# q and k loads in 2 KB packets, turned into token order, and a recorded emission order, in a fused attention and FFN kernel

## The chip, the cores and the metric

The kernel runs on one core of a Trainium2 chip. The metric is the device time of one execution in microseconds (us). The time before is 300.6 us, the median of three runs (299.19, 300.60 and 301.54 us).

A core has five instruction streams that matter here: PE (TensorE, matrix products; PEld is its weight load), DVE (VectorE), ACT (ScalarE), POOL (GpSimd) and SP (SyncE, which here only issues DMAs). Each stream is carried out in the order in which the program emits it; streams wait for each other by semaphores.

## The reference

Attention with a choice of key chunks, then an RMS norm and a gated FFN. Inputs q, k, v are (4, 8, 768, 64) float32: 4 batches, 8 heads, 768 tokens, 64 features.

```python
k_chunks = k.reshape(B, H, nc, 32, D)                 # nc = 24 chunks of 32 tokens
k_min = np.min(k_chunks, axis=3); k_max = np.max(k_chunks, axis=3)
ub = np.sum(np.maximum(q[:, :, :, None, :] * k_min[:, :, None, :, :],
                       q[:, :, :, None, :] * k_max[:, :, None, :, :]), axis=-1)
ub = np.where(causal_by_chunk, ub, -1000000000.0)
top_chunks = np.argsort(ub, axis=-1)[..., -6:]        # six chunks per query
scores = scale * np.matmul(q, k.transpose(0, 1, 3, 2))
scores = np.where(sel & causal, scores, -1000000000.0)
attn = softmax(scores)
out = np.matmul(attn, v)                              # then (B*S, H*D) = (3072, 512)
...
xn = x / rms * rms_g
g = xn @ w_gate                                       # (512, 1536)
silu = g * (1.0 / (1.0 + np.exp(-g)))
return (silu * (xn @ w_val) @ w_out)                  # (1536, 512)
```

## The kernel before

**Tiling.** The 3072 tokens are cut into 12 blocks of 256: a pair (b, m) of batch and place in the sequence, taken in the order of the list `ORDER` ((0,0), (1,0), (2,0), (3,0), (0,1), (1,1), (0,2), (2,1), (1,2), (3,1), (2,2), (3,2)). The eight heads are two groups g of four. A block is attended in two jobs (one for each g) and then passes through the FFN in six pieces of 256 hidden columns, for its 256 rows.

**A job.** SP loads k and q of a block (`load_qk`, issued in line 528) into `kraw` and `qraw`: four heads lie on the four groups of 32 partitions, and a partition holds eight tokens. DVE turns each 32x32 square (line 794, `STREAM_TRANSPOSE`) so that features lie on partitions: `kT`, `qT`. ACT or POOL makes bf16 copies `kb`, `qb` (`half`, lines 801 and 802). DVE takes the smallest and the largest of each chunk (`ext`, line 809, into `kx`). For blocks with m > 0, four DMAs issued by SP cross halves of `qT` into `QX` (line 864); `relu` (line 888) writes into the used `qraw`. PE makes the upper bounds (`upper`, lines 680 and 698), DVE finds the sixth largest and the mask (lines 723 to 755). PE makes scores (line 922) and adds the mask by a product with `chunkrow` (line 933), ACT takes exp (line 972), POOL cuts the triangle (line 942), PE multiplies by v (`values`, line 998), and DVE normalises (lines 1013, 1017).

**Norm and FFN.** ACT squares (line 1034), POOL makes the inverse root (lines 1040, 1042). For the first four blocks PE transposes x; for the other eight a DMA transposition issued by SP does (line 1058, `xsT<-xs`). PE multiplies by `wg` and `wv` (line 1122), ACT takes tanh and copies (lines 1129, 1141), DVE and POOL multiply (lines 1133, 1137, 1144), PE projects with `wo` (line 1169), and the result is stored by SP (line 1191).

**Two layouts of a load.** Blocks 0 to 2 of `ORDER` are in the set `PACKED`: a partition gets eight tokens that follow each other in memory, one packet of 2 KB per head; four loads of 128 KB for k and four for q. The turn then leaves the tokens out of order in `kT` and `qT` (position j*32 + r holds token 8r + j), and `half`, `ext`, `relu` and `upper_first` read or write with strides to set that right. In the other nine blocks partition r gets the tokens j*32 + r, in packets of 256 bytes: eight loads of 64 KB for k and eight for q, and `kT`, `qT` are in token order.

**The order of the work.** The functions do not emit at once. They make operations (`plan.op`) with an engine or a choice of engines (`flex`), an occupancy and a latency in us, and what they read, write and take from a pool of buffers. `Plan.run` then places them: at each step it takes the operation that can start first on its engine, by the due times in the list `DUE`, with a model of the DMA queues in the class `Rings`; buffers of some pools are taken in a fixed order. Where PE would stand idle in the first 60 us of the plan it adds products whose result is not used (`keep_busy`, line 1245), 77 with 128 columns and 39 with 512. Each engine's stream, SP's too, is emitted in the order that comes out. The first weight loads wait for `dk(0, 0, 0)`; the loads of block 2 and 3 wait for parts of the weights (`HELD`).

Of the kernel before, what the change touches and what calls it, by code (L numbers as in the profile page):

```python
# [19 lines left out]


# [15 lines left out]
class Rings:  # L37
    FETCHED = 3.3

    def __init__(self):  # L40
        self.now = 0.0
        self.queue = {}
        self.wait = []

    def _step(self, until):
        while True:
            heads = [q[0] for q in self.queue.values() if q]
            nxt = self.wait[0][0] if self.wait else None
            if not heads:
                if nxt is None or nxt > until:  # L50
                    return
                self.now = max(self.now, nxt)
            else:
                cycle = sum(d[1] for d in heads)
                end = self.now + min(d[0] for d in heads) * cycle
                stop = min(end, until, nxt if nxt is not None else end)
                if stop > self.now:
                    for d in heads:
                        d[0] -= (stop - self.now) / cycle
                    self.now = stop  # L60
                for q in self.queue.values():
                    if q and q[0][0] <= 1e-9:
                        q[0][2](self.now)
                        q.pop(0)
            while self.wait and self.wait[0][0] <= self.now + 1e-12:
                _, ring, d = self.wait.pop(0)
                ahead = sum(x[0] * x[1] for x in self.queue.get("POOL", ()))
                if ring != "POOL" and not d[3] and ahead > 0.0 and not self.queue.get(ring):
                    d[3] = True
                    self.wait.append((self.now + min(self.FETCHED, ahead), ring, d))  # L70
                    self.wait.sort(key=lambda w: w[0])
                    continue
                self.queue.setdefault(ring, []).append(d)
            if self.now >= until and not (self.wait and self.wait[0][0] <= until):
                if not any(q and q[0][0] <= 1e-9 for q in self.queue.values()):
                    return

    def add(self, t, ring, packets, cost, op):
        self._step(min(t, self.wait[0][0]) if self.wait else t)

        def landed(now, op=op):
            op.done = now + (0.9 if op.dma[2] else 1.2) + op.slack
        op.done = None
        self.wait.append((t, ring, [packets, cost, landed, False]))
        self.wait.sort(key=lambda w: w[0])
        self.guess()

    def room(self, ring, t):

        other = Rings()  # L90
        other.now = self.now
        other.queue = {r: [list(d) for d in q] for r, q in self.queue.items()}
        other.wait = [(w, r, list(d)) for w, r, d in self.wait]
        for q in list(other.queue.values()) + [[d for w, r, d in other.wait]]:
            for d in q:
                d[2] = lambda now: None

        def held():
            return sum(d[0] for d in other.queue.get(ring, ())) + sum(
                d[0] for w, r, d in other.wait if r == ring)  # L100

        while held() > 85.0:
            t = max(t, other.now) + 0.25
            other._step(t)
        return t

    def guess(self):
        other = Rings()
        other.now = self.now
        other.queue = {r: [list(d) for d in q] for r, q in self.queue.items()}  # L110
        other.wait = [(t, r, list(d)) for t, r, d in self.wait]
        other._step(1e9)


class Plan:

    SHARES = ("qx", "scale", "relu", "bd0", "bd1", "dk", "mk")
    PATIENT = {"DVE": 0.6, "ACT": 0.6}  # L120
    STICK = 25
    RESERVED = ("hh",)
    HOP = {"PE": 0.055, "ACT": 0.04, "DVE": 0.04, "POOL": 0.075, "SP": 0.06}

    DUE = (
        150, 162, 271, 116, 142, 170, 90, 156, 806, 900, 1138, 1422, 80, 161, 167, 163, 185, 185, 186, 186,
        187, 187, 187, 188, 12, 188, 188, 189, 200, 190, 191, 192, 194, 195, 80, 79, 85, 84, 91, 91, 95,
        122, 165, 161, 180, 195, 185, 190, 210, 214, 111, 218, 286, 225, 234, 140, 157, 160, 172, 180, 183,
        185, 155, 154, 146, 162, 202, 209, 216, 219, 216, 136, 173, 177, 183, 197, 201, 202, 206, 208, 212,
        225, 175, 178, 201, 203, 219, 229, 224, 241, 232, 235, 242, 278, 282, 19, 199, 223, 230, 235, 241,  # L130
        245, 248, 252, 240, 188, 191, 196, 202, 258, 264, 274, 278, 244, 254, 257, 282, 293, -22, 275, 280,
        299, 315, 299, 307, 323, 344, 340, 392, 213, 221, 233, 251, 249, 260, 361, 341, 333, 240, 266, 265,
        276, 294, 304, 321, 272, 291, 251, 280, 305, 310, 322, 305, 389, 293, 306, 297, 318, 320, 337, 346,
        -18, 341, 349, 401, 323, 308, 317, 470, 353, 364, 343, 392, 408, 441, 428, 418, 429, 441, 315, 328,
        336, 357, 360, 22, 358, 398, 405, 328, 327, 343, 367, 373, 385, 401, 411, 413, 417, 429, 428, 436,
        469, 414, 433, 427, 444, 395, 431, 380, 363, 357, 376, 576, 426, 404, 409, 419, 438, 456, 451, 445,
        512, 467, 476, 525, 510, 514, 463, 421, 466, 501, 417, 502, 797, 489, 379, 503, 514, 423, 411, 515,
        454, 474, 479, 484, 489, 488, 491, 506, 565, 500, 515, 501, 523, 523, 539, 514, 560, 542, 552, 561,
        472, 408, 414, 515, 518, 530, 522, 537, 575, 549, 505, 557, 567, 572, 590, 578, 597, 592, 607, 565,
        564, 571, 610, 678, 683, 641, 903, 465, 468, 490, 495, 500, 458, 507, 512, 518, 520, 530, 536, 541,  # L140
        267, 548, 553, 573, 588, 547, 819, 573, 585, 615, 619, 621, 609, 653, 567, 778, 591, 597, 607, 623,
        625, 588, 654, 618, 622, 605, 683, 682, 637, 772, 707, 760, 777, 729, 737, 736, 747, 744, 761, 784,
        786, 770, 793, 795, 660, 763, 867, 768, 791, 753, 792, 813, 818, 797, 823, 829, 900, 807, 792, 862,
        870, 883, 1080, 598, 559, 563, 569, 574, 579, 584, 659, 667, 676, 682, 688, 693, 629, 704, 711, 843,
        874, 711, 755, 727, 732, 704, 758, 864, 738, 721, 790, 738, 750, 770, 741, 798, 764, 1009, 740, 796,
        804, 745, 823, 852, 1096, 780, 891, 889, 792, 875, 892, 1020, 1031, 969, 980, 1000, 992, 1006, 1002,
        1013, 1024, 1022, 1247, 1055, 1026, 1130, 1060, 1079, 1030, 1042, 1046, 1051, 1052, 1044, 1055,
        1066, 1077, 1083, 1090, 1085, 1094, 1101, 1111, 1117, 1126, 1136, 1151, 1143, 1163, 726, 732, 738,
        744, 748, 759, 767, 773, 811, 766, 817, 827, 833, 838, 848, 854, 1028, 1044, 817, 955, 811, 871,
        945, 912, 1085, 956, 835, 954, 855, 903, 947, 845, 959, 934, 1179, 960, 998, 1009, 975, 987, 1027,  # L150
        1030, 1015, 1028, 1034, 1040, 1060, 1067, 1080, 1181, 1090, 1104, 1180, 1130, 1186, 1138, 1147,
        1158, 1193, 1217, 1219, 1193, 1372, 1222, 1225, 1186, 1194, 1217, 1213, 1222, 1222, 1002, 1251,
        1261, 1268, 1273, 1266, 1281, 1282, 1257, 1324, 1288, 1311, 1321, 1318, 1333, 864, 879, 895, 903,
        910, 828, 930, 936, 955, 964, 976, 987, 860, 1002, 1008, 1021, 1211, 1242, 980, 1107, 996, 1006,
        943, 1089, 1269, 1088, 990, 1134, 1018, 1027, 1070, 1072, 1064, 1219, 1075, 1080, 1122, 1134, 1128,
        1158, 1164, 1170, 1183, 1223, 1224, 1244, 1222, 1266, 1363, 1317, 1329, 1342, 1326, 1355, 1346,
        1363, 1379, 1278, 1294, 1306, 1387, 1326, 1441, 1405, 1453, 1450, 1452, 1380, 1373, 1433, 1407,
        1437, 1416, 1429, 1440, 1455, 1478, 1488, 1504, 1518, 1525, 1510, 1531, 1539, 1565, 1574, 1536,
        1594, 1633, 1586, 1627, 1040, 1038, 1038, 1033, 1041, 1047, 1053, 1059, 1064, 1075, 1086, 1092,
        1103, 1098, 1109, 1115, 1460, 1455, 1084, 1415, 1110, 1122, 1147, 1159, 1319, 1167, 1104, 1364,  # L160
# [94 lines left out]
    def run(self, in_order=(), fill=None):  # L255
# [19 lines left out]
        def offer(o):  # L275
            for e in o.alts:
                cand[e].append(o)
# [1001 lines left out]
```

## Time and profile before

| | |
|---|---|
| median of 3 runs | 300.6 us |
| span of the profiled execution, first to last instruction | 297.4 us |
| granted TensorE clock, mean | 0.997 |
| first product that is not fill, last PE product | at 9.15 us, at 293.7 us |
| DMA packets, under 512 B of them | 86388, 74816 |
| DMAs issued by SP | 262 |

The span is one profiled execution. No other time is given for that execution; the median of the timed runs lies 3.2 us above its span. A number such as "128x512" is partitions by elements. Busy time of an engine is the time in which an instruction runs; the ends of PE's products are modelled, so a busy PE is not always at its peak rate. "Waited for" names what came last before an engine went on; a wait for several semaphores is put down to one of them.

### The profile page before, as it was taken

To read this page: it belongs to the slowest core of one execution; us is meant where nothing else is said; L and a number is where in the kernel's file an instruction comes from. 1 tells how busy PE (TensorE), PEld (TensorE's weight loads), DVE (VectorE), ACT (ScalarE), POOL (GpSimd) and SP (SyncE) were. 2 spreads that over 40 slices of the span, in tenths; PEclk is the share of its full clock that TensorE was granted. 3 is DMA by queue.
4 is the path that set the end of the run, shared out by engine and by line. 5 is a ranking of instruction groups with operands and counts; after the bars stand their busy time and mean duration, and the time that the engine had idled before them with its cause. 6 is when DMAs were issued, how large, how long until landed. Compare 5 with 4: busy or idle time off the path is not lost.

```text
span 297.4 us, 11418 instructions
## 1 busy us (share of the span) xinstructions
PE 282.5 (95%) x4672; PEld 213.4 (72%) x4672; DVE 217.1 (73%) x623; ACT 216.7 (73%) x372; POOL 155.6 (52%) x266
## 2 busy tenths in 40 slices
PE   7879999999999996999999999899999999999994
PEld 7548777657858854878767787488688778678763
DVE  6987774977998998888999999679356454456430
ACT  4897877688979876987985797677587668565331
POOL 4885858755976864475583276538044114214120
PEclk9999999999999999999999999999999999999998
DMA  7999998755676656654768576511014021011011
GB/s 188 208 204 206 255 197 163 159 130 134 141 194 154 144 136 103 149 100 110 205 135 162 108 193 150 133 40 39 0 57 55 1 82 30 2 73 35 2 71 71
DMA packets 86388, 35.08 MB, mean 118 GB/s; under 512 B 74816, under 2 KB 81728, under 8 KB 86336
## 3 DMA queue, kind: packets, MB, share of 16 engines
q1 hardware_dynamic: 80736, 29.12, 42.6%
q0 software_dynamic: 4752, 4.72, 9.4%
q8 instruction: 36, 0.59, 0.8%
q10 hardware_dynamic: 848, 0.53, 0.7%
q14 instruction: 16, 0.13, 0.2%
HBM read 28.58 MB, written 6.29 MB: 117 GB/s over the span
## 4 chain that ended last, share of the span: by engine, by line
PE 76%; DMA 9%; DVE 4%; ACT 4%; SPq 3%; POOL 1%; issue 1%; DVEq 0%; POOLq 0%; ACTq 0%
PE F L1122 39%; PE F L1169 18%; PE S L922 6%; PE F L998 6%; PE F L680 3%; SPq L528 3%; PE S L933 2%; DMA xsT<-xs 2%; DMA qraw<-in_q_dram 2%; DMA vraw<-in_v_dram 2%; DMA kraw<-in_k_dram 2%; DVE kx L809 1%; POOL hh L1144 1%; DVE m L739 1%; ACT th L1129 1%
## 5 line engine op out<-in xcount | busy, mean ns | idle before, releaser
L972 ACT ACTIVATE pt<-S 128x1024 bf16<-128x1024 f32 (+3 forms) x104 | 85.6, 857 | 19.7 <-PE S L933 18.2
L1144 POOL TENSOR_TENSOR hh<-tg,vs 128x512 bf16<-128x512 bf16 x48 | 55.7, 1164 | 42.6 <-ACT vs L1141 22.9
L1133 DVE SCALAR_TENSOR_TENSOR tg<-th,F 128x512 bf16<-128x512 bf16 x72 | 48.4, 680 | 39.3 <-ACT th L1129 33.7
L1122 PE MATMUL F<-xsT,wg 128*128 128x256 bf16 (+1 forms) x608 | 72.6, 267 | 3.7 <-DVE xnat L1017 1.7
L1122 PE MATMUL F<-xsT,wv 128*128 128x256 bf16 (+1 forms) x608 | 72.4, 267 | 0.6 <-DMA xsT<-xs 0.3
L1169 PE MATMUL F<-wo,hh 128*128 128x512 bf16 (+1 forms) x300 | 68.5, 371 | 1.8 <-POOL hh L1144 0.6
L1122 PEld LDWEIGHTS <-wg 128*128 128x128 bf16 x608 | 55.6, 98 | 13.5 <-issue 2.7
L1122 PEld LDWEIGHTS <-wv 128*128 128x128 bf16 x608 | 55.2, 98 | 9.7 <-DMA vraw<-in_v_dram 0.8
L1129 ACT ACTIVATE th<-F 128x512 bf16<-128x512 f32 x72 | 42.5, 598 | 19.7 <-PE F L1122 17.4
L942 POOL TENSOR_SCALAR_AFFINE_SELECT pt<-pt 128x512 bf16<-128x512 bf16 x48 | 32.2, 674 | 32.3 <-ACT pt L972 31.7
L1169 PEld LDWEIGHTS <-hh 128*128 128x128 bf16 x300 | 27.7, 98 | 28.4 <-issue 1.8
L1141 ACT ACTIVATE vs<-F 128x512 bf16<-128x512 f32 x48 | 28.7, 598 | 13.2 <-PE F L1122 10.1
L922 PE MATMUL S<-qb,kb 32*128 32x256 bf16 (+1 forms) x800 | 32.8, 253 | 2.3 <-ACT qb L801 2.0
L809 DVE TENSOR_REDUCE kx<-kT 128x16 f32<-128x512 f32 x48 | 30.4, 664 | 0.0
L998 PEld LDWEIGHTS <-pt 128*128 128x128 bf16 x672 | 24.8, 98 | 3.1 <-issue 0.3
L998 PE MATMUL F<-VX,pt 128*128 128x65 bf16 x672 | 26.6, 194 | 0.2 <-ACT vs L1141 0.2
L922 PEld LDWEIGHTS <-kb 32*128 32x128 bf16 x800 | 13.9, 92 | 15.0 <-issue 14.4
L933 PE MATMUL S<-mtd,chunkrow 32*128 32x128 bf16 (+2 forms) x384 | 20.5, 203 | 0.2 <-issue 0.2
L933 PE MATMUL S<-mto,chunkrow 32*128 32x128 bf16 (+2 forms) x384 | 19.9, 203 | 0.0
L1017 DVE TENSOR_TENSOR xnat<-F,rden 128x256 bf16<-128x256 f32 x48 | 19.2, 415 | 0.7
L933 PEld LDWEIGHTS <-chunkrow 32*128 32x128 bf16 x768 | 18.5, 93 | 1.2 <-issue 0.4
L1034 ACT ACTIVATE junk<-xnat 128x512 bf16<-128x512 bf16 x24 | 15.1, 631 | 5.4 <-DVE xnat L1017 5.0
(71 smaller groups left out, 337.2 us busy)
## 6 DMA issues: line engine op xcount, KB each, us to landing
vraw<-in_v_dram SPq DMA_DIRECT2D x24, 256.0 KB, 4.4
out_dram<-osb SPq DMA_DIRECT2D x23, 256.0 KB, 2.4
kraw<-in_k_dram SPq DMA_DIRECT2D x72, 64.0 KB, 2.4
qraw<-in_q_dram SPq DMA_DIRECT2D x72, 64.0 KB, 2.2
QX<-qT SPq DMA_DIRECT2D x32, 64.0 KB, 2.7
wg<-in_moe_w_gate_dram POOLq DMA_DIRECT2D x3, 512.0 KB, 12.3
wv<-in_moe_w_val_dram POOLq DMA_DIRECT2D x3, 512.0 KB, 14.3
wo<-in_moe_w_out_dram POOLq DMA_DIRECT2D x3, 512.0 KB, 23.5
```

What stands on the lines that cost most here:

```text
L809: plan.op(f"ext{n}{J}", "DVE", 0.585, 0.67, lambda n=n, op=op: VE.tensor_reduce(out=at(kx)[:, g, n], in_=at(kT).rearrange("p h (j c x) -> ...
L922: TE.matmul(s[a // 2][:, a % 2, c0:c0 + q1 - q0], kbt[r, t, ks], qbt[r, t, q0:q1], start=(t == 0), stop=(t == 1 and not mask), skip_group_ ...
L933: TE.matmul(o, chunkrow[r, BLK * kg + P * e:BLK * kg + P * (e + 1)], mv, start=False, stop=(d == 1), skip_group_check=True)
L942: GE.affine_select(out=d, in_=d, compare_op=ALU.is_ge, fill=0.0, base=0, pattern=[[0, 4], [1, P]], channel_multiplier=-1)
L972: lambda pt=pt, hs=hs, c0=c0, c1=c1, x=sc[hp]: SE.activation(out=at(pt)[:, hs, c0:c1], in_=at(x)[:, :, c0:c1], func=ACT.Exp, scale=SCALE), ...
L998: TE.matmul(o[:, a, :], p_[:, a, off:off + P], vt[:, e, a, :], start=(kb_ == 0 and a == 0), stop=(kb_ == nkb - 1 and a == 3), skip_group_c ...
L1122: TE.matmul(at(p_)[:, n * W:(n + 1) * W], w[:, g, ht * P:(ht + 1) * P], at(xT)[:, g, x0:x0 + W], start=(g == 0), stop=(g == NP - 1), skip_ ...
L1129: plan.op(f"tanh{U}.{hp}", "ACT", 0.48, 0.6, lambda th=th, gp=gp: SE.activation(out=at(th), in_=at(gp), func=ACT.Tanh, scale=0.5), pri - 0 ...
L1133: VE.scalar_tensor_tensor(out=at(tg), in0=at(th), scalar=1.0, in1=at(gp), op0=ALU.add, op1=ALU.mult), pri - 30, reads=[th, gp], writes=[tg ...
L1141: plan.op(f"vcopy{U}.{hp}", "ACT", 0.48, 0.6, lambda vs=vs, vp=vp: SE.activation(out=at(vs), in_=at(vp), func=ACT.Copy), pri + 0.1, reads= ...
L1144: plan.op(f"hh{U}.{hp}", "POOL", 1.11, 1.16, lambda tg=tg, vs=vs, hh=hh: GE.tensor_tensor(out=at(hh), in0=at(tg), in1=at(vs), op=ALU.mult) ...
L1169: TE.matmul(at(op)[:, cs], at(key)[:, o:o + P], wo[:, ht, cs], start=(ht == 0), stop=(ht == NHT - 1), skip_group_check=True)
```

## The change

Three things change.

1. `PACKED` is gone: all 12 blocks load q and k in the layout with 2 KB packets, in four loads of 128 KB each (before: three blocks). Counted over the program, loads of q and k go from 168 to 96, and SP's DMAs from 262 to 190.
2. The turn writes its output with a stride of 8 elements (32 bytes), so that `kT` and `qT` are in token order. The strided accesses of `half`, `ext`, `relu` and `upper_first` go; these now read and write in order.
3. `Rings`, `DUE` and the placing are gone. A list `SEQUENCE` gives the order of all 1508 operations (1580 before), `SLOTS` the buffer of each, `CHOICE` the engine of each `flex` operation, and `WARM` where fill goes: again 77 products with 128 columns and 39 with 512. Some occupancies are other numbers than before; nothing reads them any more in the changed kernel.

In the emitted streams, 73 `flex` operations change their engine; the net change is 6 more operations on DVE, 3 fewer on ACT, 3 fewer on POOL. PE's 315 operations are the same, in another order: 55 stand at the same place, 141 within three places of it. The changes between PE's kinds of operation (FFN and values, scores, upper bounds) go from 121 to 132.

```diff
+SEQUENCE = [
+    34, 19, 35, 3, 37, 36, 33, 0, 21, 6, 23, 32, 16, 31, 8, 4, 1, 38, 7, 17, 25, 30, 9, 15, 40, 10, 18, 42, 20,
...
+SLOTS = [
...
+CHOICE = (
...
+WARM = [
+    (60, 77, 0, 0), (72, 4, 0, 1), (99, 6, 0, 1), (120, 8, 2, 1), (126, 2, 2, 1), (135, 4, 3, 1), (146, 2, 0,
+    1), (158, 2, 3, 1), (174, 1, 2, 1), (242, 6, 3, 1), (258, 4, 1, 1)]
...
-    PACKED = {0, 1, 2}
...
-            if i in PACKED:
-                sv = src[b].rearrange("(g a) (m r j) d -> a m r g (j d)", a=4, m=NBLK, r=32)[a, m]
-                todo = [(sv, lambda rows=rows: at(key)[rows].rearrange("r g j h d -> r g (j h d)"),
-                         4, 0.104 if i == 0 else 0.12)]
-            else:
-                todo = []
-                for g in range(NG):
-                    sv = src[b, 4 * g + a, BLK * m:BLK * (m + 1), :].rearrange(
-                        "(j r) d -> r j d", r=32)
...
+            sv = src[b].rearrange("(g a) (m r j) d -> a m r g (j d)", a=4, m=NBLK, r=32)[a, m]
+            dma(f"load {nm}{b}{m}{a}", eng, sv,
+                lambda rows=rows: at(key)[rows].rearrange("r g j h d -> r g (j h d)"),
...
-                    lambda: VE.transpose(out=turned(nm).rearrange("p h (j r) -> p j h r", r=32, j=8),
+                    lambda: VE.transpose(out=turned(nm).rearrange("p h (r j) -> p j h r", r=32, j=8),
                                          in_=at(raw)[:, g]),
...
-            act = lambda: SE.activation(out=natural(at(hb)), in_=order(turned(nm)), func=ACT.Copy)
-            pool = lambda: GE.tensor_copy(natural(at(hb)), order(turned(nm)))
+            act = lambda: SE.activation(out=at(hb), in_=turned(nm), func=ACT.Copy)
+            pool = lambda: GE.tensor_copy(at(hb), turned(nm))
...
-                out=at(kx)[:, g, n], in_=at(kT).rearrange("p h (j c x) -> p h c j x", j=8, x=4)
-                if packed else at(kT).rearrange("p h (c t) -> p h c t", t=CH),
-                axis=AXXY if packed else AXX, op=op), base + 1, reads=[kT, kT + (g,)] + ([kx] if n or g else []), writes=[kx + (g, n)],
+                out=at(kx)[:, g, n], in_=at(kT).rearrange("p h (c t) -> p h c t", t=CH),
+                axis=AXX, op=op), base + 1, reads=[kT, kT + (g,)] + ([kx] if n or g else []), writes=[kx + (g, n)],
...
-    for o in plan.run(in_order=("kraw", "qraw", "vraw", "kT", "qT", "kb", "qb", "QX", "VX", "xsT", "xs", "hh", "xnat"),
-                      fill=(1.6, 5.6, 60.0, 0.0565, 0.216, "F", keep_busy)):
+    for o in plan.run(("F", keep_busy)):
         o.fn()
```

In the new order SP issues the four DMAs of line 864 for block (1, 1) one right after the other, directly before the loads of block (2, 1), and the first DMA transposition (line 1058) stands behind 118 DMAs (before: 138).

## Prediction

> **What bounds the kernel now.** First the page: how busy each engine is, and where. These are the busy times, then PE's and the DMAs' rows of the span in 40 slices, then the chain that ended last.
>
> ```profile
> PE 282.5 (95%) x4672; PEld 213.4 (72%) x4672; DVE 217.1 (73%) x623; ACT 216.7 (73%) x372; POOL 155.6 (52%) x266
> ...
> PE   7879999999999996999999999899999999999994
> ...
> DMA  7999998755676656654768576511014021011011
> ...
> PE 76%; DMA 9%; DVE 4%; ACT 4%; SPq 3%; POOL 1%; issue 1%; DVEq 0%; POOLq 0%; ACTq 0%
> ```
>
> PE bounds it: 76% of the chain, and no other engine is near 95%. The change takes no product away from PE, so it can only win time in which PE waits or does fill. The view by stretches says where that is (columns: length, then busy us of PE, PEld, DVE, ACT, POOL; clock; DMA share).
>
> ```profile
> 9.00:60.00 51.00, 47.98 (x827) 35.10 (x829) 39.11 (x123) 41.55 (x86) 39.05 (x69) 1.00 1.06 198
> 60.00:140.00 80.00, 75.44 (x1357) 57.29 (x1356) 69.96 (x230) 66.93 (x119) 52.21 (x76) 1.00 0.59 136
> 140.00:195.00 55.00, 54.13 (x1064) 39.53 (x1062) 49.45 (x152) 43.78 (x70) 29.83 (x52) 1.00 0.66 149
> 195.00:294.00 99.00, 98.48 (x1363) 75.22 (x1354) 52.10 (x110) 59.52 (x95) 30.14 (x36) 1.00 0.14 39
> 75.00:187.50 112.50, 108.08 (x2041) 81.95 (x2038) 104.21 (x330) 92.03 (x154) 71.34 (x111) 1.00 0.64 144
> ```
>
> PE's idle time is 51.00 - 47.98 = 3.0 us at first, 4.6 us from 60 to 140, 0.9 us and 0.5 us after that: 9.0 us in all. In the first stretch it also makes 39 wide fill products; five that follow each other take 1.24 us with 0.38 us for the last, so 0.215 us each and 8.4 us in all. The pool is thus some 17 us, half of it fill that the changed program makes again (39 of the same size). From 195 us on there is nothing to win. The clock is full throughout.
>
> What holds PE in the second stretch is read from the chain between 100 and 136 us.
>
> ```profile
> 104.72 0.59 SPq L864
> 105.37 0.58 SPq L528
> ...
> 108.46 0.45 SPq L528
> 108.96 0.59 SPq L864
> 109.59 0.59 SPq L864
> 110.23 2.06 DMA QX<-qT
> 112.53 0.62 POOL qraw L888
> 113.20 1.15 PE F L680 x45
> ...
> 131.32 3.72 DMA xsT<-xs
> ```
>
> SP's queue is in it: between the first and the last of four crossings (line 864) SP issues six loads of q, then the crossings land, POOL makes relu, and PE stands idle 0.4 us before line 680. The two DMA transpositions are issued behind all that, from 112.08 to 114.7 us, and at 117.58 us PE begins line 1122 after 1.7 us idle (the profile's list names DVE there, but the weight load of the same products waited for `xsT<-xs`). At 135.1 us the next transposition is late too.
>
> **Part 1: fewer and larger loads.** 72 DMAs of SP go. A load's issue takes 0.449 us (median of 82 for k), so 72 x 0.449 = 32 us of SP's time between 40 and 175 us, in which the timeline shows SP issuing almost without a pause. Crossings, transpositions and stores behind loads go out sooner, and SP's order puts the crossings of block (1, 1) together. The price: a load of 64 KB lands 2.4 us after its issue, one of 128 KB 5.3 us, though that figure is from the start, with a DMA share of 1.06. At a share of 0.6 I take 3 us; loads stand many microseconds ahead of their turn, so it costs nothing unless a turn follows closely (+1 us at most, for two such places). Gain: bounds 0 (the waits come back elsewhere) and the 4.6 + 0.9 us of idle time in these stretches. I take 3.5 us, most of it, because 0.4 + 1.7 us of it hang on SP by the chain, and the smaller ones at 129.8 and 135.1 us follow the late transposition.
>
> **Part 2: the copies read in order.** In blocks 0 to 2 the twelve copies to bf16 read with a stride of 128 bytes. One view by source line gives the prices (minimum/median/maximum ns).
>
> ```profile
> L801 ACT ACTIVATE kb<-kT x14: 612/637/1115, 5.8 to 163.7; 128x512 bf16<-128x512 f32 x14
> L801 ACT ACTIVATE qb<-qT x8: 610/1083/1147, 8.0 to 113.9; 128x512 bf16<-128x512 f32 x8
> ...
> L794 DVE STREAM_TRANSPOSE qT<-qraw x24: 668/694/712, 7.3 to 176.8; 128x512 f32<-128x512 f32 x24
> ...
> L809 DVE TENSOR_REDUCE kx<-kT x48: 642/672/687, 6.3 to 185.3; 128x16 f32<-128x512 f32 x48
> ```
>
> The strided ones are the 1083 ns, the others 637 ns: 0.446 us less each. On the path lie the one before the first scores (9.15 us, PE had waited 1.06 us for it) and the three between 15 and 22.5 us, where ACT is busy 7.50 of 7.50 us. Bounds: 0.45 us (the first alone) and 4 x 0.446 = 1.8 us. I take 1.0 us: the fill stays in PE's stream, and DVE's chain to the first norm is not shortened. The loads of block 3 (issued from 40 to 53 us) go from packets of 256 bytes to an eighth as many, but between 40 and 60 us PE hardly idles: 7.50 and 7.46 of 7.50 us in the two stretches from 45 us on. Nothing for that. `ext`, with one or two free axes, has 642 to 687 ns in both layouts: nothing.
>
> **Part 3: the turn writes with a stride of 32 bytes.** The trace has no such turn. Its nearest rows: `ext` reads pieces of 16 bytes, 128 bytes apart, at the price of plain reading; and DVE's small memset (line 730) writes float32 with a step of 136 bytes, 16 of them in 72 ns against 2 in 60 ns, so 12 / 14 = 0.86 ns an element, less than the turn's 694 / 512 = 1.36 ns. By these the cost is 0. The other bound is ACT's stride, 0.446 us a turn. Nothing suggests a gain, since the reading side is unchanged. I take 0, for the memset is DVE's own writing with a larger step.
>
> [...]
>
> **Part 4: the order.** PE's kinds of work change 132 times instead of 121. In the trace line 922 begins 0.10 us later after line 1122 than the latter's spacing of 0.110 us would give (100.26 against 99.83 + 3 x 0.110). So 11 x 0.10 = 1.1 us more. Six operations move to DVE net, most of them `dk` (0.325 us there): 2 us of DVE, hidden while it has 8.3 us to spare in 75 to 187.5 us. The last products (the projection of block 11 in halves) stand as before, so the tail is kept. New waits of the order: between -1 and +5 us, from the pool's 9.0 us of idle time that the old order left; I take 0, as most PE operations stand within three places.
>
> **Sum.** 297.4 - 3.5 - 1.0 + 0 + 1.1 + 0 = 294.0 us of span; with the 3.2 us by which the median lies above the span, 297.2 us. Two of the bounds lie further down than up of what I took (0.9 us more of idle time, 0.8 us of ACT), so I put the forecast a little lower, at 296.7 us.
>
> **The rivals.** *The moves cancel.* PE is at 95%, its fill is the same, and each wait removed may stand again a few products later, in the new order. For it: after 140 us PE idles only 1.4 us, so nearly all must come from the 4.6 us before. Then 300.6 + 1.1 - 1.0 gives 300.7 us, from 298.5 to 303.
>
> *DVE becomes the bound (slower).* If a turn costs 0.446 us more, the four of block 0 stand before the first bounds and scores: 4 x 0.446 = 1.8 us. From 75 to 187.5 us there are 28 turns: 12.5 us more, against DVE's idle time of 112.5 - 104.2 = 8.3 us, so at least 4.2 and at most 12.5 us. With the 3.4 us of the sum's gain off, 300.6 - 3.4 + 6.0 = 303.2 to 300.6 - 3.4 + 14.3 = 311.5 us. It decides from 8.3 / 28 = 0.30 us a turn on. For it: ACT's row; DVE is 93% busy in that stage. Against it: the memset and `ext`.
>
> *The relief is larger.* If SP's queue also caused what is put down to DVE and ACT between 60 and 100 us and half of the start's waits, up to 9.0 us of idle time goes: 300.6 - 9.0 + 1.1 = 292.7 us.
>
> **How the numbers follow.** Forecast 0.40 (294.5 to 298.5 us), larger relief 0.12 (290.5 to 294.5), moves cancel 0.26, DVE the bound 0.22. About 1%, 3 us, is what a measurement of this kernel can tell from no change. Faster by over 1% (below 297.6 us): 0.33 of the forecast and 0.12 make 0.45. Slower by over 1% (above 303.6 us): 0.21 of DVE and 0.04 of the moves make 0.25. Within 1%: 0.30. The range reaches from 291 to 306 us: it leaves out the lowest of the relief and the upper half of the DVE case. The forecast's own range is 294.5 to 298.5 us.
>
> **What would show it.** Line 801 at 0.64 us in all rows; line 794 still near 0.69 us (at 1.0 us or more the slower rival is right); SP with 190 DMAs and pauses between 60 and 175 us; no idle time of PE over 0.5 us before lines 680 and 1122 between 100 and 140 us; PE's idle time from 60 to 195 us near 2 us instead of 5.5 us. It would be wrong if PE's idle time there is unchanged, or if loads that land later than 3 us hold up turns.

## The result, and the profile after

The changed kernel takes 310.6 us (median of 4 runs, 309.6 to 312.4), the kernel before 299.9 us beside it (299.1 to 301.5). The ratio is 1.033, with a 95% interval from 1.027 to 1.039. It is slower by some 10 us; the forecast was 296.7 us. The profiled execution has a span of 309.2 us.

The page first, with the rows shown of before and DVE's row in the 40 slices.

```profile
PE 288.0 (93%) x4672; PEld 216.8 (70%) x4672; DVE 237.3 (77%) x628; ACT 210.5 (68%) x367; POOL 155.3 (50%) x263
...
PE   8599989979999988898799999999999999999994
...
DVE  7689986999998999999989999984635643645251
...
PEclk9879999988999999999999999999999999999999
...
PE 52%; DVE 29%; DMA 8%; issue 4%; ACT 3%; SPq 2%; POOL 1%; DVEq 0%; ACTq 0%; POOLq 0%
```

DVE's row and the row of the clock that TensorE was granted (PEclk, in tenths) were these before:

```profile
DVE  6987774977998998888999999679356454456430
...
PEclk9999999999999999999999999999999999999998
```

DVE has taken over: its share of the chain that ended last goes from 4% to 29%, at PE's cost, and it is at nine tenths in most slices up to the 26th. Two dents in PEclk are new, at slices 2 and 3 and at 9 and 10. The view by stretches shows the same in us (columns: length, then busy us of PE, PEld, DVE, ACT, POOL; clock; DMA share; GB/s).

```profile
9.00:60.00 51.00, 46.39 (x783) 33.25 (x783) 43.99 (x121) 36.29 (x76) 34.52 (x59) 0.93 1.07 204
60.00:140.00 80.00, 74.14 (x1280) 55.41 (x1279) 76.79 (x229) 63.90 (x117) 54.25 (x87) 0.98 0.71 172
140.00:195.00 55.00, 50.55 (x914) 37.93 (x912) 52.20 (x137) 40.19 (x65) 29.09 (x46) 1.00 0.32 82
```

From 60 to 195 us DVE is busy 129.0 of 135 us (before: 119.4), and PE idles 10.3 us where it idled 5.4 us. What DVE does more is read from the view by source line (minimum/median/maximum ns).

```profile
L594 DVE STREAM_TRANSPOSE kT<-kraw x24: 1079/1102/1167, 5.2 to 186.0; 128x512 f32<-128x512 f32 x24
L594 DVE STREAM_TRANSPOSE qT<-qraw x24: 1070/1096/1122, 10.1 to 179.0; 128x512 f32<-128x512 f32 x24
...
L601 ACT ACTIVATE qb<-qT x10: 630/630/668, 11.3 to 188.1; 128x512 bf16<-128x512 f32 x10
```

Line 594 is the turn, line 794 of before. It takes 1.10 us where it took 0.69 us: 0.41 us more, 48 times, is 19.7 us of DVE. ACT's copies are at 0.63 us throughout, as Part 2 said. The list of PE's waits between 9 and 195 us names the same engine (columns: us in total, times, longest).

```profile
PE S L717 <- ACT qb L601: 4.0, 2, 3.7
PE F L917 <- DVE tg L928: 3.1, 5, 0.9
PE F L917 <- DVE xnat L812: 1.9, 2, 1.1
PE F L506 <- DVE tg L928: 1.4, 1, 1.4
PE F L917 <- DVE xsT L886: 1.0, 1, 1.0
```

Only the first row is another matter: the first scores stand at 11.95 us instead of 9.15 us. In the new order ACT's table load (1.28 us, from 1.72 us on) stands ahead of ACT's two loads of q, which go out at 4.08 instead of 1.73 us. I had not looked at ACT's queue at the start when I costed the order.

### The profile page after: what moved, and what is told of

Its sections match the earlier page's. It is cut to its first block, busy times and chain, and to the rows that moved or that the text cites. A ratio compares the mean times of both kernels' runs of the same rounds, so it can differ in the third digit from the quotient of the medians.

```text
span 309.2 us, 11305 instructions
## 1 busy us (share of the span) xinstructions
PE 288.0 (93%) x4672; PEld 216.8 (70%) x4672; DVE 237.3 (77%) x628; ACT 210.5 (68%) x367; POOL 155.3 (50%) x263
## 4 chain that ended last, share of the span: by engine, by line
PE 52%; DVE 29%; DMA 8%; issue 4%; ACT 3%; SPq 2%; POOL 1%; DVEq 0%; ACTq 0%; POOLq 0%
PE F L917 25%; PE F L964 14%; DVE qT L594 5%; DVE kT L594 5%; PE S L717 4%; PE F L793 4%; DVE kx L609 4%; DVE tg L928 4%; DMA kraw<-in_k_dram 3%; DVE xnat L812 2%; DVE xs L847 2%; DMA qraw<-in_q_dram 2%; SPq L349 2%; DMA vraw<-in_v_dram 2%; PE S L728 1%
## 5 line engine op out<-in xcount | busy, mean ns | idle before, releaser
L939 POOL TENSOR_TENSOR hh<-tg,vs 128x512 bf16<-128x512 bf16 x48 | 56.8, 1189 | 44.5 <-DVE tg L928 25.8
L964 PE MATMUL F<-wo,hh 128*128 128x512 bf16 (+1 forms) x300 | 69.9, 376 | 1.7 <-DVE tg L928 0.9
L964 PEld LDWEIGHTS <-hh 128*128 128x128 bf16 x300 | 28.3, 99 | 28.9 <-issue 4.2
L737 POOL TENSOR_SCALAR_AFFINE_SELECT pt<-pt 128x512 bf16<-128x512 bf16 x48 | 30.7, 648 | 16.3 <-ACT pt L767 16.0
L717 PE MATMUL S<-qb,kb 32*128 32x256 bf16 (+1 forms) x800 | 33.5, 255 | 4.2 <-ACT qb L601 4.0
L793 PEld LDWEIGHTS <-pt 128*128 128x128 bf16 x672 | 25.8, 98 | 6.2 <-issue 2.3
L793 PE MATMUL F<-VX,pt 128*128 128x65 bf16 x672 | 28.3, 194 | 1.7 <-DVE xnat L812 0.8
L594 DVE STREAM_TRANSPOSE qT<-qraw 128x512 f32<-128x512 f32 x24 | 24.4, 1094 | 2.5 <-DMA qraw<-in_q_dram 2.5
L594 DVE STREAM_TRANSPOSE kT<-kraw 128x512 f32<-128x512 f32 x24 | 25.0, 1105 | 0.7 <-DMA kraw<-in_k_dram 0.5
L932 DVE TENSOR_TENSOR hh<-tg,F 128x512 bf16<-128x512 bf16 x24 | 16.3, 683 | 7.6 <-PE F L917 7.1
## 6 DMA issues: line engine op xcount, KB each, us to landing
wv<-in_moe_w_val_dram POOLq DMA_DIRECT2D x3, 512.0 KB, 10.7
```

The source lines that it names most:

```text
L594: lambda: VE.transpose(out=turned(nm).rearrange("p h (r j) -> p j h r", r=32, j=8), in_=at(raw)[:, g]),
L717: TE.matmul(s[a // 2][:, a % 2, c0:c0 + q1 - q0], kbt[r, t, ks], qbt[r, t, q0:q1], start=(t == 0), stop=(t == 1 and not mask), skip_group_ ...
L737: GE.affine_select(out=d, in_=d, compare_op=ALU.is_ge, fill=0.0, base=0, pattern=[[0, 4], [1, P]], channel_multiplier=-1)
L793: TE.matmul(o[:, a, :], p_[:, a, off:off + P], vt[:, e, a, :], start=(kb_ == 0 and a == 0), stop=(kb_ == nkb - 1 and a == 3), skip_group_c ...
L939: plan.op(f"hh{U}.{hp}", "POOL", 1.11, 1.16, lambda tg=tg, vs=vs, hh=hh: GE.tensor_tensor(out=at(hh), in0=at(tg), in1=at(vs), op=ALU.mult) ...
L964: TE.matmul(at(op)[:, cs], at(key)[:, o:o + P], wo[:, ht, cs], start=(ht == 0), stop=(ht == NHT - 1), skip_group_check=True)
```

## Experiments

Two theories stood at the beginning: (1) the strided turn alone makes the loss, through DVE; (2) the new order makes a good part of it, by what it puts late and by how it packs the engines. All ratios are to the kernel before, run beside each kernel on the same chip (its medians there: 300.5 to 301.7 us).

**The turn and the start of the new order.** In the first, third and fourth of these four kernels the tokens stand in another order in `kT` and `qT` than the rest of the kernel takes them to, and the output is not the reference's; the instructions are the same ones.

```diff
 e1_turn_contiguous (from the kernel after)
-out=turned(nm).rearrange("p h (r j) -> p j h r", r=32, j=8)
+out=turned(nm).rearrange("p h (j r) -> p j h r", r=32, j=8)
 e2_q_loads_first (from the kernel after): the three operations 38, 39 and 41
 of SEQUENCE (loads of q) moved ahead of operation 1 (the table load)
 e3_both: e1 and e2 together
 e4_before_strided (from the kernel before): e1's edit the other way round
```

> The changed kernel with one edit: the turn writes each square in one piece, as before the change, so the tokens of a block lie in another order in kT and qT than the rest of the kernel takes them to, and the output is another; every instruction and its place is the same. Theory 1 (the strided turn, 1.10 us instead of 0.69 us, 48 x 0.41 = 19.7 us of DVE, is what costs after the start): the lag that the changed kernel gathers after 60 us (about 7.7 of its 11.7 us) goes, and the time is 301 to 303 us. Theory 2 (the new order itself waits more): line 594 falls to 0.69 us, but 306 us or more is left. Theory 3 (the start): a delay of 3 to 4 us is left in the first 30 us whatever the turn costs, since q arrives at 10.1 us instead of 7.3 us.

> The changed kernel with the two loads of q that ACT issues put back ahead of ACT's table load, as they stood before; the turn stays strided. Theory 3 (the start is late because these loads are issued at 4.1 us instead of 1.7 us): the first scores move from 11.9 us to about 9.5 us, PE's clock stays at 1.00 in the first 22 us, and the time falls by 2.5 to 4 us, to 307 us. If the loss at the start is hidden by what follows (DVE full from 60 to 200 us): the first scores move, but the time falls by less than 1 us.

> Both edits: the turn in one piece (tokens in another order, so another output) and q's loads ahead of the table. If turn and start are the whole loss and add up, this is the forecast of 296.7 us or what the new order is worth by itself: 296 to 300 us. If the new order is worse by itself: above 301.5 us.

> The kernel before with one edit: all 48 turns write with the stride of 32 bytes, in the old order with the old loads; the tokens of a block lie in another order than the rest takes them to, so the output is another. Theory 1: line 794 goes from 0.69 to 1.10 us and the time rises by 6 to 14 us (1.8 us at the start and at least 28 x 0.41 - 8.3 = 3.2 us in the stretch from 75 to 187.5 us), to 307 to 314 us. If DVE's slack or PE's fill hides it: under 303 us, and the loss of the changed kernel is the order's.

Measured: e1 298.6 us (0.993, 0.990 to 0.996), e2 309.2 us (1.029, 1.023 to 1.035), e3 299.5 us (0.998, 0.994 to 1.001), e4 305.6 us (1.017, 1.012 to 1.022). With the contiguous turn the changed kernel stands 0.7% below the one before: undoing one access pattern takes 12.0 us off. The same pattern put into the kernel before costs 5.1 us there, less than I had expected. The late start is no part of the loss that lasts: e2 brings the first scores to 9.2 us, and its time is shorter by 1.4 us, which is within the intervals; e3 wins nothing against e1. In e3's trace PE stands idle between 60 and 65 us instead, and the clock falls there (windows as above).

```profile
60.00:62.50 2.50, 1.37 (x64) 1.38 (x65) 2.30 (x3) 2.50 (x6) 2.40 (x3) 1.00 0.98 310
62.50:65.00 2.50, 1.76 (x12) 0.92 (x12) 2.50 (x8) 1.33 (x4) 1.38 (x2) 0.73 1.10 224
65.00:67.50 2.50, 2.50 (x8) 0.90 (x7) 2.42 (x12) 1.73 (x4) 1.43 (x3) 0.59 1.32 224
```

From 62.5 us on PE's own products run at 0.73 and then 0.59 of the clock, just behind 1.9 us of idle time. In e1's trace PE idles 0.2 us between 60 and 65 us, with the same kinds of products, and the clock stays at 1.00.

**The order alone, the clock, half of the turns, the stride by itself.** The second kernel keeps e3's output order; in the third q is not in token order. e5 gives the reference's output.

```diff
 e5_order_alone (from the kernel after): contiguous turn, strided copies in
 blocks 0 to 2, and from block 3 on per load
-DMA: src "(g a) (m r j) d -> a m r g (j d)"        (128 KB, packets of 2 KB)
+two DMAs: src[b, 4 * g + a] "(j r) d -> r j d"     (64 KB, packets of 256 bytes)
 e6_fill_gap (from e3): 5 fill products into a score bank ahead of place 410
 (upper of block 3), 3 ahead of place 419 (norm transposition)
 e7_k_turns_strided (from the kernel after)
+rearrange("p h (r j) -> p j h r" if nm == "k" else "p h (j r) -> p j h r", ...)
 e8_probe_strides (from the kernel before), behind its end, four times each:
+VE.transpose(out=by(dst_, n), in_=by(src_, 1))     # n = 1, 2, 4, 8, 16
+VE.transpose(out=by(dst_, 1), in_=by(src_, 8))
+VE.tensor_copy(...)                                # 1; write 4, 8; read 8
+VE.memset(by(dst_, n), 0.0)                        # n = 1, 8
+by(x, n) = x.rearrange("p (a r b) -> p a b r", r=32, b=n)
```

> The new emission order alone: the kernel after, but q and k come in the packets of the kernel before (256 bytes from the fourth block on, two loads of 64 KB where the kernel after has one of 128 KB) and are turned with the contiguous write; the output is the reference's. Against the contiguous-turn run (298.6 us, 2 KB packets) only packet size and number of loads differ. Theory A (the packets carry the gain of 3.5 us that the prediction took for them): 301.5 to 303 us, PE idle of about 5 us again in 60 to 195 us. Theory B (the new order carries it, the packets are covered anyway): 298 to 299.5 us, PE idle there near 2.7 us as in the contiguous-turn run.

> The run with contiguous turn and the q loads first (299.5 us) plus 8 wide fill matmuls into an idle score bank: 5 before the pooled scores of the block whose issue left PE idle 1.2 us at 60 us, 3 before the next norm transposition (0.83 us idle at 62.5 us). Theory A (the granted clock of 0.73 and 0.59 at 62 to 67 us in that run follows from PE standing still there, and costs about 1.5 us: 5 us at 0.79 and 3.1 busy us at 0.87): clock 0.95 or more at 60 to 70 us and 297.5 to 298.5 us. Theory B (the clock falls for another reason, or DVE takes back what PE wins): clock still under 0.9 there, or time 299 to 300.5 us.

> The kernel after with only the 24 turns of k written in token order (32-byte step), those of q contiguous (q is then not in token order). Between 298.6 us (none strided) and 310.6 us (all 48). Theory A (DVE has spare time that takes up the first part, and only what exceeds it is paid; 24 x 0.41 = 9.8 us of DVE, of which 16 or 17 turns, about 7 us, lie in 60 to 195 us, where the contiguous-turn run has 7.6 us of DVE idle): at most a third of the whole price, 299 to 302.5 us. Theory B (each turn stands on the path of its block, so the price goes by the number of turns): half of it, 303.5 to 306 us.

> The kernel before with 48 instructions of VectorE after its end, on one buffer of 128 x 512 fp32: turns of 32x32 blocks written with a step of 1, 2, 4, 8 and 16 elements, one read with a step of 8, copies written with a step of 1, 4 and 8 and one read with 8, and memsets with a step of 1 and 8. The time is not compared. Theory A (price per element written to another 32-byte piece, whatever the operation): turn 0.65 us at step 1, rising with the step to 1.1 us at 8 (full from a step of 4 or 8 elements on), and copy and memset rise in the same way at step 8. Theory B (a price of the turn alone): turn as above, copy and memset equal at every step, as the memset row that the prediction argued from. The strided read of the turn tells whether it is the write side only: 0.65 to 0.7 us if so.

Measured: e5 323.1 us (1.071, 1.068 to 1.074), e6 298.9 us (0.991, 0.987 to 0.994), e7 304.1 us (1.010, 1.007 to 1.012).

e5 missed both expectations by 20 us: the new order with the old loads is by far the slowest of the kernels that are compared. From 41 to 80 us its SP issues loads almost without a pause, and SP is in the chain (the page's chain row).

```profile
PE 62%; SPq 9%; DMA 9%; DVE 6%; POOL 5%; ACT 4%; issue 3%; ACTq 0%; DVEq 0%; POOLq 0%
```

SP has 72 issues more, at about 0.45 us each, than the changed kernel, and between 56 and 81 us the chain runs through these issues and the landings of k and v. It seems that the new order puts the loads where only the shorter queue brings them in time, so in this run order and loads can't be judged apart. The granted clock is also lower, 0.94 between 60 and 195 us, and this part of the loss was not separated. Packets of 256 bytes in loads of 128 KB were not tried, so the number of loads and the size of the packets stay unseparated.

e6 holds the clock at this place: 1.00 and PE busy 2.50 of 2.50 us in all five windows from 57.5 to 70 us. Its ratio is 0.7% (2.1 us) under e3's, which agrees with a dip that costs some 1.5 us (the estimate in e6's expectation, from the clocks of 0.87 and 0.79 in e3); but the intervals overlap a little, and the spans of the profiled executions (298.9 and 298.1 us) don't show it. e6's has a pause of its own: at 28.9 us PE waits 3.0 us for `VX`, which waited for a load of v, and the clock is 0.59 and 0.73 in the two windows from 32.5 to 37.5 us; the mean clock of both executions is 0.994. Of e3's ten executions the two with a mean clock of 0.999 are the shortest (298.0 and 298.5 us; the others, at 0.986 to 0.994, take 299.0 to 302.1 us), but a longer pause, such as e6's 3.0 us ahead of its 0.59, can lengthen the time and lower the clock alike. So the clock is shown at that place, and its price is not.

e7 pays 41% of the way from e1 to the kernel after (0.0165 of 0.0403) for half of the turns. That lies between the third that theory A allowed and the half of theory B, and nearer to the third; its 304.1 us lie in theory B's range. So e7 does not settle whether a turn is paid where it delays its own block or where the sum of all turns fills DVE.

e8's view of VectorE by source line; columns are busy us, mean ns. Lines 1258 to 1262 are turns written with a step of 1, 2, 4, 8 and 16 elements, 1263 a turn read with 8, 1264 a plain copy, 1265 and 1266 copies written with 4 and 8, 1267 a copy read with 8, 1268 and 1269 memsets with 1 and 8.

```profile
L1261 DVE STREAM_TRANSPOSE kT<-qraw 128x512 f32<-128x512 f32 x4 | 4.4, 1097 | 0.1
L1263 DVE STREAM_TRANSPOSE kT<-qraw 128x512 f32<-128x512 f32 x4 | 4.4, 1092 | 0.1
L1260 DVE STREAM_TRANSPOSE kT<-qraw 128x512 f32<-128x512 f32 x4 | 4.3, 1078 | 0.1
L1262 DVE STREAM_TRANSPOSE kT<-qraw 128x512 f32<-128x512 f32 x4 | 4.1, 1034 | 0.1
L1266 DVE COPY kT<-qraw 128x512 f32<-128x512 f32 x4 | 2.5, 626 | 0.1
L1267 DVE COPY kT<-qraw 128x512 f32<-128x512 f32 x4 | 2.5, 623 | 0.1
L1265 DVE COPY kT<-qraw 128x512 f32<-128x512 f32 x4 | 2.5, 622 | 0.1
L1258 DVE STREAM_TRANSPOSE kT<-qraw 128x512 f32<-128x512 f32 x3 | 2.1, 712 | 0.1
L1259 DVE STREAM_TRANSPOSE kT<-qraw 128x512 f32<-128x512 f32 x3 | 2.1, 712 | 0.1
L1268 DVE MEMSET kT<- 128x512 f32 x4 | 1.9, 485 | 0.7 <-DVE kT L1267 0.7
L1269 DVE MEMSET kT<- 128x512 f32 x4 | 1.9, 485 | 2.2 <-DVE kT L1268 2.2
L1264 DVE COPY kT<-qraw 128x512 f32<-128x512 f32 x4 | 1.7, 427 | 0.1
```

The step of 2 elements (8 bytes) is free, 712 ns as with 1. From 4 elements (16 bytes) on the turn takes 1.03 to 1.10 us, whichever side is strided, and a copy 0.62 instead of 0.43 us (the reading side was tried with a step of 8 only, and the copy not with 2). A memset takes 485 ns either way. Turn and copy pay on either side; the memset, which only writes, does not and says nothing of them. That is theory A for turn and copy, and theory B for the memset alone. Written with two elements to each 16 bytes (step of 2) the turn keeps its 712 ns; with one (step of 4) it pays in full, 1078 ns.

**Loads and order, taken apart.** In the second kernel the tokens of blocks 3 to 11 are in another order, so its output is not the reference's.

```diff
 e9_copies_reorder (from the kernel after): turn contiguous; readers strided
+half: out=natural(at(hb)), in_=order(turned(nm));  relu: x = order(x)
+upper: at(qx)[:, g].rearrange("p h (x j c r) -> p h c j r x", x=8, j=4, c=2)
 e10_old_order_loads (from the kernel before), blocks 3 to 11
-two DMAs per quarter: "(j r) d -> r j d"
+one DMA, in the first one's place: "(g a) (m r j) d -> a m r g (j d)"
 e11_old_order_all: e10, and the turns, copies, bounds and relu of the kernel after
 e12_reorder_q_first: e9 with e2's and e6's edits
```

> The kernel after (its order, its 2 KB loads), with the reordering taken off VectorE's turn: the turn writes contiguously, and the copies to bf16 (ACT, POOL), relu and the pooled-score products read with the stride of 128 bytes, as the kernel before does in blocks 0 to 2; the output is the reference's. 48 copies at 0.446 us more are 21 us for ACT and POOL together, and 48 turns at 0.41 us less 20 us less for DVE. Theory A (DVE is what binds, ACT and POOL have room): 298 to 301 us, near the contiguous-turn run's 0.993 of before. Theory B (the copies stand on the path to the scores of each block): 303 to 308 us.

> The kernel before in its own emission order, but with q and k of blocks 3 to 11 in the 128 KB loads of 2 KB packets of the kernel after (72 loads fewer; each stands where the first of its two halves stood); turns and copies as before, so those blocks' tokens are in another order in the output. Theory A (the gain of 3.5 us that the prediction took for fewer and larger loads is there in any order): 0.983 to 0.993 of the kernel before, 296 to 299 us. Theory B (the order recorded for small loads has already hidden them; they matter only in the new order, which issues its loads later): 0.995 to 1.003.

> Everything that the change does to the data (2 KB loads, turns written in token order with the 32-byte step, copies and relu read in order), in the emission order of the kernel before; the output is the reference's. Theory A (the parts add: the old-order run with strided turns paid 1.7%, the loads give back what the run beside this one shows, the twelve copies about 1 us): 1.00 to 1.012 of before, 301 to 304.5 us, and then the new order, not the data, makes most of the loss at 1.033. Theory B (the strided turn costs the same 4% once the loads are those of the change): 1.025 to 1.035.

> The run with the reordering in the copies, and besides the q loads of the first block ahead of the table load and the 8 fill products at 60 and 62 us; the output is the reference's. If the pieces add as in the contiguous-turn runs (0.993 alone, 0.9905 with both): 0.25 to 0.5% below the run with the reordering in the copies alone, and faster than both kernels, 296.5 to 300 us. If the copies bind: no better than that run.

Measured: e9 309.6 us (1.030, 1.025 to 1.034), e10 296.2 us (0.984, 0.980 to 0.988), e11 302.4 us (1.006, 1.004 to 1.009), e12 308.2 us (1.025, 1.019 to 1.030). The larger loads do win, 4.9 us in the old order. e11 then shows that all of the data's change is worth a loss of 1.3 us in the old order; together with the new order it is the whole change, a loss of 10.7 us.

e9 and e12 are misses on the bad side: taking the stride off DVE and giving it to the readers costs as much. The list of groups shows POOL's part of it (busy us, mean ns, idle before).

```profile
L707 POOL TENSOR_SCALAR qraw<-QX 128x512 f32<-128x512 f32 x16 | 17.8, 1128 | 2.8 <-DMA QX<-qT 2.5 <-issue 0.3
L621 POOL CAST kb<-kT 128x512 bf16<-128x512 f32 x14 | 14.9, 1084 | 7.8 <-DVE kT L613 7.8
```

And the view of line 500, the pooled-score products:

```profile
L500 PE MATMUL F<-QX,BD x256: 376/393/418, 84.9 to 197.0; 64*32 64x128 f32 x128
L500 PE MATMUL F<-qraw,BD x256: 266/278/296, 85.3 to 197.3; 64*32 64x128 f32 x128
```

POOL's relu goes from 626 to 1128 ns, its copies from 614 to 1084 ns (first figures: e1), and PE itself reads the strided `QX` at 393 ns a product, beside 278 ns for a product of the same shape from a plain buffer. Which of these e9 pays for is not shown: from 60 to 195 us DVE is busy 122.6 us in it, ACT 107.1 and POOL 102.3 us of 135.

**Pairs.** If two elements to each 16 bytes are enough in reading too, as they are in e8's written turn (712 ns, and 1078 ns with one), the reordering of k can be split into two steps that both keep two tokens together. Both kernels give the reference's output.

```diff
 e13_k_in_pairs (from e10): q of blocks 3 to 11 turned as in the kernel after, k:
+turn: out=flat(kT) "p (x h r y) -> p x y h r", x=4, h=2, y=2   # step of 2
+half: in_=flat(kT) "p (x hr y) -> p hr x y", x=4, y=2          # reads pairs
+ext:  in_=flat(kT) "p (x h c z) -> p h c x z", x=4, h=2, z=8
 e14_k_by_copies: the same, but k turned contiguously and its copies reading
 single elements ("p h (j r) -> p h r j")
```

> The old order with the 2 KB loads (0.984 of before with tokens out of order), made to give the reference's output: in blocks 3 to 11 the 18 turns of q write in token order with the 32-byte step, and the 18 of k write pairs (step of 8 bytes, two elements to each 16 bytes) into a buffer in which two neighbouring tokens stay together; the copies of k to bf16 and the chunk bounds then read pairs. Blocks 0 to 2 as before. Theory A (what costs is one element per 16 bytes, so both halves of the split reordering are free, as the probe's 712 ns for a step of 2 elements says of the write): turns of k 0.69 to 0.72 us, their copies 0.61 to 0.70 us, and the time pays for 18 turns x 0.41 = 7.4 us of VectorE only, of which about 8 us of its idle time takes up most: 0.984 to 0.993 of before, 296 to 299 us, faster than both kernels. Theory B (every step over 4 bytes costs, in the reading at least): copies of k near 1.08 us, 0.993 to 1.005.

> As the run beside it, but k of blocks 3 to 11 is turned contiguously and its copies to bf16 read single elements 128 bytes apart, as in blocks 0 to 2 of the kernel before. Theory A (copies with one element per line cost 0.45 us more each on ACT or POOL, 18 of them, and stand before the scores): 0.3 to 1% slower than the run with k in pairs. Theory B (ACT and POOL have room in the old order, so it is hidden): within 0.2% of it.

"One element per line" means the single reads, 128 bytes apart.

Measured: e13 297.8 us (0.989, 0.985 to 0.993), e14 298.4 us (0.991, 0.988 to 0.994). Both stand below both kernels, about 1% below the one before. Their copies by source line, e13's first, with its turn of k (busy us, mean ns, idle before):

```profile
L818 ACT ACTIVATE kb<-kT x14: 643/672/1103, 5.8 to 162.9; 128x512 bf16<-128x512 f32 x14
L819 POOL CAST kb<-kT x10: 623/638/1042, 37.7 to 181.9; 128x512 bf16<-128x512 f32 x10
...
L812 DVE STREAM_TRANSPOSE kT<-kraw 128x512 f32<-128x512 f32 x24 | 16.1, 693 | 0.6 <-DMA kraw<-in_k_dram 0.6
```

```profile
L811 ACT ACTIVATE kb<-kT x14: 1082/1102/1125, 5.7 to 163.5; 128x512 bf16<-128x512 f32 x14
L812 POOL CAST kb<-kT x10: 1052/1078/1092, 37.4 to 182.9; 128x512 bf16<-128x512 f32 x10
```

Reading pairs costs ACT 0.67 us instead of 1.10, and POOL 0.64 instead of 1.08 (e13's maxima are blocks 0 to 2, which read singly). The turns of k in e13 take 0.69 us on average. So two elements to 16 bytes are enough, or nearly so (plain copies take 0.63 and 0.61 us in e1), in the kernel as in the probe. That the copies' 0.43 us are worth anything to the time is not shown: 0.2% lies between the two, inside both intervals.

## Why the prediction was wrong, point by point

**Part 3 failed**, "The other bound is ACT's stride, 0.446 us a turn ... I take 0, for the memset is DVE's own writing with a larger step." This is the step that failed. The turn costs 0.41 us more, almost that other bound, and with e1 against the changed kernel the 48 of them are worth 12.0 us of the time where the sum had 0. The memset was DVE's own writing, but the wrong neighbour: e8 shows memset free at the same step at which turn and copy pay. The small rows of 2 and 16 elements had nothing to do with it; with 512 elements the memset is free too. `ext` was the wrong neighbour as well: it read pieces of 16 bytes, four elements each, where by e8 and e13 two are enough, while the turn writes one element to each. ACT's row with one element per 128 bytes (1083 ns, and 637 ns in order) was the one of the turn's kind, and the sum set it aside for the memset.

**The slower rival was right**, in mechanism, and in size partly by luck (303.2 to 311.5 us; the time is 310.6). Of the other groups of instructions with over 10 us of busy time none has a mean more than 2% longer in the kernel after than in e1, so what is paid is VectorE's time. The clock can explain little of it: its mean is 0.983 in the kernel after and 0.988 in e1, and the dent at the start stands in e1 too (0.50 from 14.5 to 19.5 us); only the second dent is the kernel after's own. The price depends on how much of VectorE's idle time was left. These are the rows for 60 to 195 us of e10 and e11, the old order without and with the strided turn:

```profile
60.00:195.00 135.00, 130.71 (x2456) 99.43 (x2462) 121.30 (x387) 111.70 (x189) 83.28 (x127) 1.00 0.54 133
```

```profile
60.00:195.00 135.00, 127.69 (x2312) 96.02 (x2322) 129.45 (x382) 109.48 (x187) 82.97 (x129) 1.00 0.54 131
```

and of e1 and the kernel after, the same in the new order:

```profile
60.00:195.00 135.00, 132.29 (x2471) 98.94 (x2470) 127.39 (x407) 109.01 (x189) 86.31 (x130) 1.00 0.54 133
```

```profile
60.00:195.00 135.00, 124.69 (x2191) 93.34 (x2190) 128.99 (x365) 104.10 (x181) 83.34 (x132) 0.99 0.55 136
```

DVE's idle time is 13.7 us in e10 and 5.6 us in e11, so the old order takes up 8.1 us; turns in this stretch take 13.1 us more (34.6 against 21.5 us by the same windows for the turn's line), which leaves 5.0 us, and 6.2 us were measured (e11 also has the copies in order). In the new order it is 7.6 and 6.0 us: only 1.6 us are taken up of 13.3 us (33.6 against 20.3 us), which leaves 11.7 us, and 12.0 us were measured. Some 6 us of idle time remain in either, and no run has less than e11. The rival's spare 8.3 us, read from the old trace, is near what the old order took up in this longer stretch; that the new order would have used 6.1 us of it before the turn came was the point that neither rival nor forecast saw. There the luck lies: for the old order the rival's 6.0 to 14.3 us are too much for e4 (5.1 us) and at their low end for e11 (6.2 us over e10). The fit is arithmetic over shifted windows, not an experiment of its own, and a rough one: for e4 it leaves 4.9 us, but for e7, whose turns take 6.9 us more than e1's while DVE idles 8.0 us, it leaves some 7 us, and 5.0 to 5.5 us were measured.

**Part 1's size was right, a little small:** 3.5 us taken, 4.9 us measured in the old order (e10). Its mechanism is shown in part. PE's idle time from 60 to 195 us is 135 - 132.3 = 2.7 us in e1, near the 2 us that was named as the sign, but in e10 it is 4.3 us, only 1.1 us less than before; where e10 wins the rest is open.

**Part 2's prices were right** (0.63 us in all rows of ACT). Its 1.0 us was not measured by itself.

**Part 4 was too small and too simple.** 1.1 us were taken for the switches and 0 for new waits. With contiguous turns and new loads the new order stands 0.9% above the old one, 0.993 against 0.984 and so about 2.7 us (e1 also reads the copies of blocks 0 to 2 in order), inside the bounds; its missed wait, q's loads behind the table load, costs 2.8 us at the first scores and, by e2 and e3, little or nothing at the end. With strided turns the order costs 2.7%, or 8.1 us (1.033 against 1.006). The parts did not add, though the prediction's sum supposed that they would:

| ratio to the kernel before | old loads | new loads, turn contiguous | new loads, turn strided |
|---|---|---|---|
| old order | 1 | 0.984 (e10) | 1.006 (e11) |
| new order | 1.071 (e5) | 0.993 (e1) | 1.033 (the change) |

With the old order, the old loads and strided turns it is 1.017 (e4).

Why the new order leaves DVE less idle time with the same turns is only partly seen: six more operations on DVE are about 2 us by the prediction, but e1's DVE is busy 6.1 us more than e10's in that stretch and has 407 instructions there against 387, so there is more to it. Over the whole execution e1's DVE is busy 222.3 us and e10's 216.8: e1's has 2.5 us more before 60 us and 3.1 us less behind 195 us. So about half of the 6.1 us is work brought forward from behind the stretch, and the rest is more work on DVE (the largest part: ten operations of line 614 instead of five, 2.2 us).

**The last step of the sum** has no ground in its bounds either. "Two of the bounds lie further down than up" holds for Part 2; Part 1's 3.5 us stand 2.0 us from the bound of more gain (5.5 us) and 3.5 us from the bound of none. The 0.5 us so taken off are small beside the 12.0 us.

## What to carry to other kernels

When an operation's access pattern changes and the trace lacks it, take its price from rows with the same number of elements per 16 bytes (e8's turn: 0.71 us with two, 1.03 to 1.10 us with one or fewer), of operations that read as well as write (e8's memset took 485 ns at a step of 1 and of 8), and if such rows disagree, let the dear one set the forecast. Before an engine is given more work, look at its idle time in the order that will run, not in the one that ran. A recorded order can depend on the loads it was recorded with: e5, the new order with the old loads, lost 7%. It need not: e10 and e13 show that the larger loads pay at once in the old order.

## What the runs showed of the hardware

- In the turns and copies run here one fp32 element to each 16 bytes or more cost time; two cost nothing or little. VectorE's turn took 0.71 us with two and 1.08 us with one (e8, the written side); ACT's copy to bf16 takes 0.67 and 1.10 us, POOL's 0.64 and 1.08 us (e13 and e14, the side read; plain 0.63 and 0.61 us in e1). VectorE's copy takes 0.43 us in plain order and 0.62 us with one (e8). A memset of 512 elements takes 485 ns at a step of 1 and of 8 (e8).
- In e9 PE's products of 128 columns from an fp32 operand read with a step of 128 bytes took 393 ns, and 278 ns from a plain one.
- The granted clock fell to 0.59 in e3 behind two pauses of PE of only 1.20 and 0.83 us, and with e6's eight fill products it was 1.00 there. In e6 it fell to 0.59 elsewhere, behind one pause of 3.0 us, and in the kernel after it was 0.50 from 14.5 to 19.5 us, behind the pause of 3.7 us. But pauses of 1.43 and 0.56 us between 28 and 31 us left it at 1.00 in e3, so no limit can be read from these runs.
